# Retention, then a swish MLP, on one core: batch 0 in two-position runs and 64x64 tiles, its keys ahead of its values

## The chip, the cores and the metric

The kernel runs on one core of a Trainium2 chip. TensorE (PE) multiplies matrices out of SBUF into PSUM; VectorE (DVE) and ScalarE (ACT) read PSUM; GpSimd (POOL) works on SBUF alone; SyncE (SP) issues most of the DMAs. Each engine takes its instructions in order. The metric is device time in microseconds, the median of several runs. The profile shows one execution.

## What is computed

```python
scores = scale * np.matmul(q, k.transpose(0, 1, 3, 2))
gamma = 1.0 - 2.0 ** (-5.0 - np.arange(H, dtype=np.float32))
rel = pos[:, None] - pos[None, :]
Dmat = np.where(rel >= 0, gamma[:, None, None] ** rel[None, :, :], 0.0)
attn = np.matmul(scores * Dmat[None], v)
x = attn.transpose(0, 2, 1, 3).reshape(B * S, H * D)
h = x @ w_in
out = (h * (1.0 / (1.0 + np.exp(-beta * h)))) @ w_out
```

There are 8 batches of 8 heads, 576 positions and 64 channels per head, all in float32. The decay gamma^(i-j) is a product of gamma^i on the query side and gamma^-j on the key or value side, so no decay matrix is needed, only a causal mask. `w_in` is 512 x 2048 and `w_out` 2048 x 512, 4 MB each.

## The kernel before

Each batch has four chunks of 128 positions and a tail of 64; the tails of two batches are handled together. A chunk `c` works with keys and values of 128 positions on the 128 partitions. It has scores of the chunk's queries against its keys (`a_sc`, then a masking multiplication on DVE into `R`), values weighted by `R` (`a_O`), a crossing term from the running key-value state of all earlier chunks (`a_cross`), and an update of that state (`a_st`, with two ACT copies per chunk into the block-diagonal tiles `sbds`). `a_x` copies the result `O` out of PSUM into `xT`, transposed as the MLP needs it. Before that, queries are scaled with their decay (`pre_q`, tile `qs`) and transposed on PE (`t_q`, then a copy to `qT`); keys are cast to bf16 (`pre`, tile `kn`) and transposed (`t_k`, then an ACT copy to `kT`); values are scaled with gamma^-j (`pre`, tile `vn`, on POOL).

The queries are interleaved: partition p holds positions 4p to 4p+3, so a run of 4 x 64 floats, 1 KB, lies together in memory. Keys and values have one position per partition and run, 256 bytes. The kernel's first lines issue on SP's queue the queries of batch 0 (two halves of the heads, line 80), then the eight key and value loads of batch 0 (`ahead`, line 93), then `w_in` in pieces (`load_w_in`, line 177): four 256 columns wide, two 512 wide. A piece is cast to bf16 by `cast_w_in` (line 185), partly on POOL, partly on DVE. Two 256-wide pieces share one of the four `wt` buffers. The loads of `w_out` (line 189) use these buffers again and so wait for the casts.

The MLP of a batch is 16 `up` steps (line 410: four 512-column matmuls, then a Silu on ACT) and 16 `down` steps for each of four row blocks (line 423). The order of all work is written out by hand. First comes a straight list of calls for batch 0's attention, from line 454 on, with `warm_up` matmuls between them that compute nothing used. Then `merged` walks through the list `fill` of `up` and `down` steps of all batches and puts the attention steps of later batches, the casts and the loads between them at given places (`streams`). Every engine follows this order of program.

PSUM has eight banks, shared by tags: three `mm` (MLP, `warm_up`, some others), two `sc` (scores), two `O` (outputs, and the transposes `T`), one `st` (state). A new tile of a tag waits until an old one of that tag has been read.

## Time and profile before

| what | value |
|---|---|
| median of 3 runs | 312.85 us (312.38 to 313.4) |
| the profiled execution's span, first to last instruction | 310.4 us |
| the same execution's time outside the span | not listed; the median is 2.45 us above the span |
| PE busy | 299.4 us, 96% of the span |
| ACT, DVE, POOL busy | 46%, 35%, 31% |
| chain that ended last: PE, SP's queue, DMA | 89%, 4%, 3% |
| first `up` matmul | 19.51 us |
| granted TensorE clock | 1.000 |

The chain that ended last is followed back from the last instruction; its shares say what the time hung on. A line of the list in order of time has start, duration, engine, line, operation, what it writes and reads, and in brackets how long the engine had been idle and what ended that. In the windows, each engine has its busy time in the stretch, with the number of instructions.

### The profile page before, as it was taken

Reading aid. Unit: us, or ns where it says so; the run is one execution under the profiler, and the core shown is the slowest. Engines: PE = TensorE matmul, PEld = TensorE weight load, DVE = VectorE, ACT = ScalarE, POOL = GpSimd, SP = SyncE. Lnnn points to the kernel's source line nnn. Section 1 sums busy time; section 2 is a strip of 40 time slices with the busy share of each in tenths; the row PEclk is TensorE's granted clock in tenths of the full one; section 3 lists DMA queues with packets and bytes.
Section 4 is the critical chain, followed back from the end, with each engine's and each line's share of the span. In section 5 each row is a group of like instructions: output and inputs, shape, how many; then the busy total and the mean of one; then the engine's idle time right before and its main releaser. Section 6 shows DMA issues by size and latency. Waiting matters only on the chain.

```text
span 310.4 us, 5341 instructions
## 1 busy us (share of the span) xinstructions
PE 299.4 (96%) x2142; PEld 157.3 (51%) x2177; DVE 110.1 (35%) x196; ACT 141.5 (46%) x250; POOL 96.4 (31%) x131
## 2 busy tenths in 40 slices
PE   7789999999999999999999999999999999999996
PEld 5544456765454454445544544545455454444444
DVE  6554476342433142434431434133415420010012
ACT  5577626984147502661077106720574037206700
POOL 4663026846524281362228021912420000000000
PEclk9999999999999999999999999999999999999999
DMA  7999999999979989996989598949832110041011
GB/s 202 220 354 386 380 239 269 234 233 200 234 163 170 215 183 230 230 204 98 243 228 112 120 211 224 194 100 208 195 60 50 68 70 0 9 93 37 0 67 71
DMA packets 123897, 52.79 MB, mean 170 GB/s; under 512 B 105680, under 2 KB 116320, under 8 KB 123872
## 3 DMA queue, kind: packets, MB, share of 16 engines
q1 hardware_dynamic: 98496, 46.15, 61.3%
q10 hardware_dynamic: 25376, 6.30, 13.5%
q8 instruction: 17, 0.28, 0.4%
q14 instruction: 8, 0.07, 0.1%
HBM read 36.71 MB, written 9.44 MB: 149 GB/s over the span
## 4 chain that ended last, share of the span: by engine, by line
PE 89%; SPq 4%; DMA 3%; issue 1%; DVE 1%; ACT 0%
PE po L423 40%; PE ph L410 38%; DMA wt<-in_moe_w_in_dram 3%; SPq L93 3%; PE O L364 3%; PE sc L322 3%; PE O L350 2%; PE st L393 2%; SPq L177 1%; PE T L296 1%; PE T L302 1%; DVE xT L381 0%; DVE w_in_sb L185 0%; PE O L347 0%; SPq L80 0%
## 5 line engine op out<-in xcount | busy, mean ns | idle before, releaser
L412 ACT ACTIVATE gT<-ph,beta_sb 128x512 bf16<-128x512 f32 (+1 forms) x154 | 100.4, 659 | 83.1 <-PE ph L410 82.4
L410 PE MATMUL ph<-xT,w_in_sb 128*128 128x512 bf16 (+1 forms) x599 | 128.9, 365 | 2.5 <-DVE w_in_sb L185 1.1
L423 PE MATMUL po<-w_out_sb,gT 128*128 128x512 bf16 (+2 forms) x590 | 127.4, 368 | 1.3 <-issue 0.5
L410 PEld LDWEIGHTS <-w_in_sb 128*128 128x128 bf16 x616 | 58.7, 98 | 64.3 <-DVE w_in_sb L185 2.2
L423 PEld LDWEIGHTS <-gT 128*128 128x128 bf16 x608 | 57.0, 98 | 62.3
L332 DVE TENSOR_TENSOR R<-sc,causal 128x512 bf16<-128x512 f32 x71 | 44.3, 684 | 56.5 <-PE sc L322 55.0
L430 DVE COPY ot<-po 128x512 f32<-128x512 f32 (+2 forms) x38 | 25.0, 662 | 86.2 <-PE po L423 83.4
L254 POOL TENSOR_TENSOR vn<-kvn,gv 128x512 bf16<-128x512 f32 x32 | 33.3, 1042 | 16.8 <-DMA kvn<-in_v_dram 15.5
L272 POOL CAST kn<-kvn 128x512 bf16<-128x512 f32 x32 | 19.6, 612 | 58.9 <-DMA kvn<-in_k_dram 58.5
L246 POOL TENSOR_TENSOR qs<-qn,gq 128x512 bf16<-128x512 f32 x24 | 24.3, 1042 | 27.3 <-DMA qn<-in_q_dram 27.3
L381 DVE CAST xT<-O 128x512 bf16<-128x512 f32 x30 | 19.4, 687 | 34.8 <-PE O L350 15.5
L398 ACT CAST sbd<-st 64x256 bf16<-64x256 f32 x48 | 17.5, 364 | 18.8 <-PE st L393 16.6
L398 ACT CAST end<-st 64x256 bf16<-64x256 f32 x16 | 5.9, 366 | 29.4 <-PE st L393 29.3
L393 PE MATMUL st<-vn,kn 128*128 128x128 bf16 x128 | 12.4, 220 | 0.2 <-POOL vn L254 0.2
L364 PEld LDWEIGHTS <-vn 128*64 128x64 bf16 x288 | 8.7, 110 | 6.7 <-issue 6.1
L364 PE MATMUL O<-R,vn 128*64 128x128 bf16 x288 | 11.9, 223 | 0.0
L303 ACT COPY kT<-T 128x512 bf16<-128x512 bf16 x12 | 6.9, 586 | 8.8 <-PE T L302 7.7
L393 PEld LDWEIGHTS <-kn 128*128 128x128 bf16 x128 | 9.0, 98 | 3.5
L322 PE MATMUL sc<-qT,kT 64*128 64x128 bf16 x256 | 10.3, 218 | 0.4 <-ACT kT L303 0.2
L322 PEld LDWEIGHTS <-kT 64*128 64x128 bf16 x288 | 8.1, 94 | 3.8 <-ACT kT L303 1.5
L350 PE MATMUL O<-qT,sbd 128*128 128x128 bf16 x96 | 8.3, 221 | 0.3 <-ACT xT L381 0.2
L207 PE MATMUL ph<-warm 128*128 128x128 f32 (+1 forms) x24 | 6.9, 426 | 1.2 <-DVE warm L118 1.2
(56 smaller groups left out, 85.8 us busy)
## 6 DMA issues: line engine op xcount, KB each, us to landing
qn<-in_q_dram SPq DMA_DIRECT2D x16, 512.0 KB, 5.5
kvn<-in_k_dram SPq DMA_DIRECT2D x32, 256.0 KB, 5.9
kvn<-in_v_dram SPq DMA_DIRECT2D x32, 256.0 KB, 5.7
out_dram<-ot SPq DMA_DIRECT2D x31, 256.0 KB, 2.8
wt<-in_moe_w_out_dram SPq DMA_DIRECT2D x4, 1024.0 KB, 9.5
wt<-in_moe_w_in_dram SPq DMA_DIRECT2D x4, 512.0 KB, 7.3
wt<-in_moe_w_in_dram SPq DMA_DIRECT2D x2, 1024.0 KB, 11.7
out_dram<-ot SPq DMA_DIRECT2D x9, 128.0 KB, 2.4
```

The costliest lines, as they stand in the source:

```text
L246: e.tensor_tensor(batch[b]["qs"][:, cs, hs], q_tiles[b][:, hs, cs].rearrange("p h i d -> p i h d"), gq[:, cs, hs].unsqueeze(3).to_broadcas ...
L254: nc.gpsimd.tensor_tensor(live[i]["vn"][:], kv_tiles.pop(i)[:, 1], gains(gv, c), ALU.mult)
L272: nc.gpsimd.tensor_copy(kn[:, c % 2], t[:, 0])
L322: nc.tensor.matmul(view(sc[j][:, p, :]), L["kT"][r, p, :], rhs, start=True, stop=True, skip_group_check=True)
L332: nc.vector.tensor_tensor(R[:, j], sc[j][:], causal4[:] if i == CB - 1 else m_b, ALU.mult)
L364: nc.tensor.matmul(O[j * D:(j + 1) * D, p, :], vn[:, 2 * p + j, :], R[:, j, p, :], start=p == 0 and not (early and crossed), stop=early or ...
L393: nc.tensor.matmul(st[:, p, :], heads(L["kn"], p), heads(L["vn"], p), start=(c == 0 and p == 0), stop=True, skip_group_check=True)
L398: nc.scalar.copy(s[r, :, j * D:(j + 1) * D], st[r, :, j * D:(j + 1) * D])
L410: nc.tensor.matmul(ph, w_in_sb[:, ko, fo * P:(fo + 1) * P], xts[m][:, ko, :, w], start=(ko == 0), stop=(ko == KO - 1))
L412: nc.scalar.activation(gts[m][:, fo, :, w], ph, ACT.Silu, scale=beta_sb[:, fo:fo + 1])
L423: nc.tensor.matmul(po[:, :nn], gT[:, fo, ms, :], w_out_sb[:, fo, n0:n0 + nn], start=(fo == 0), stop=(fo == FO - 1))
L430: nc.vector.tensor_copy(ot, po[:, :nn])
```

## The change

The queries of batch 0 come in halves with a quarter of the keys between them. Keys and values of batch 0 are loaded in two spans of 256 positions, two positions to a partition (512-byte runs), each in two halves of the heads: all keys first, then all values. The decay gamma^-j moves from the values to the keys of batch 0. Since a partition now holds two positions, a chunk's keys lie on 64 partitions in two layers, and scores, outputs and states of batch 0 work on half of the partitions: 64x64 tiles for scores and outputs. The order of batch 0's attention is written anew. `betas_safe` and the reciprocal move from POOL to DVE, ahead of the queries. The first 256 columns of `w_in` come in two pieces; the last state of batch 0 (`w_st(3)`) goes into the stream behind the first `up` step. The qT copies of batch 0 change between DVE and ACT. Special forms for batch 0 in `a_sc`, `a_cross` and `a_O` go. The diff, with the set-up of constants and the removed branches shortened:

```diff
-    ahead = [(0, 0), (0, 1), (1, 0), (1, 1), (2, 0), (3, 0), (2, 1), (3, 1)]
+    SP = 2 * P
+    wide = {}
+    def load_q0(u):
+        if u == 0:
+            q_tiles[0] = stage.tile([P, H, CB, D], F32, name="qn", tag="qn", bufs=2)
+        w = slice(u * HP, (u + 1) * HP)
+        nc.sync.dma_start(q_tiles[0][:, w].rearrange("p h i d -> p h (i d)"),
+                          q[0, w, :MB, :].rearrange("h (p i) d -> p h (i d)", i=CB))
+    def load_wide(s, j, u):
+        if u == 0:
+            wide[s, j] = stage.tile([P, H, 2, D], F32, name="kvn", tag="kvn", bufs=NQ)
+        w = slice(u * HP, (u + 1) * HP)
+        nc.sync.dma_start(wide[s, j][:, w].rearrange("p h i d -> p h (i d)"),
+                          (k, v)[j][0, w, s * SP:(s + 1) * SP, :].rearrange("h (p i) d -> p h (i d)", i=2))
...
-    load_q(0)
-    for n, j in ahead:
-        load_kv(n, (j,))
+    load_q0(0)
+    load_wide(0, 0, 0)
+    load_q0(1)
+    for s, j, u in ((0, 0, 1), (1, 0, 0), (1, 0, 1), (0, 1, 0), (0, 1, 1), (1, 1, 0), (1, 1, 1)):
+        load_wide(s, j, u)
...
+    nc.gpsimd.iota(pos[:, 2 * CV:], pattern=[[SP, 2], [1, 2]], base=0, channel_multiplier=2,
+                   allow_small_or_imprecise_dtypes=True)
...
-    causal4 = consts.tile([P, HP, P], BF16, name="causal4")
-    nc.gpsimd.tensor_copy(causal4[:], causal[:].unsqueeze(1).to_broadcast([P, HP, P]))
+    causal_w = consts.tile([P, 2, P], BF16, name="causal_w")
+    nc.gpsimd.memset(causal_w[:], 1.0)
+    for x in range(2):
+        for i in range(2):
+            r = slice(x * TL, (x + 1) * TL)
+            nc.gpsimd.affine_select(out=causal_w[r, i], in_=causal_w[r, i], pattern=[[1, CB], [CB, PC]],
+                                    compare_op=ALU.is_ge, fill=0.0, base=-i, channel_multiplier=-2)
...
-    pieces = [(f, 256) for f in range(0, 1024, 256)] + [(f, 512) for f in range(1024, d_ff, 512)]
+    pieces = [(0, 128), (128, 128)] + [(f, 256) for f in range(256, 1024, 256)] + [(f, 512) for f in range(1024, d_ff, 512)]
...
-            on_pool = ko == KO - 1 or g < 4 and ko > 1
+            on_pool = ko == KO - 1 or g < 5 and ko > 1
...
-        nc.gpsimd.tensor_tensor(tiny[:], beta_sb[:], beta_sb[:], ALU.mult)
-        nc.gpsimd.tensor_scalar(tiny[:], tiny[:], 1e-24, 1e-12, ALU.is_lt, ALU.mult)
-        nc.gpsimd.tensor_tensor(beta_sb[:], beta_sb[:], tiny[:], ALU.add)
+        nc.vector.tensor_tensor(tiny[:], beta_sb[:], beta_sb[:], ALU.mult)
+        nc.vector.tensor_scalar(tiny[:], tiny[:], 1e-24, 1e-12, ALU.is_lt, ALU.mult)
+        nc.vector.tensor_tensor(beta_sb[:], beta_sb[:], tiny[:], ALU.add)
+        nc.vector.reciprocal(rbeta_sb[:], beta_sb[:])
...
-        (nc.vector.tensor_copy if u else nc.scalar.copy)(batch[b]["qT"][:, :, 2 * u:2 * u + 2], T[:])
+        (nc.vector.tensor_copy if u != (b == 0) else nc.scalar.copy)(batch[b]["qT"][:, :, 2 * u:2 * u + 2], T[:])
...
+    def wide_start():
+        t = sb.tile([P, 12, HP, P], BF16, name="w0", tag="gT", bufs=2)
+        for s in range(2):
+            spans[s] = dict(
+                kn=sb.tile([P, 2, H, D], BF16, name="kn", tag="kn", bufs=4),
+                kT=sb.tile([P, 2, HP, P], BF16, name="kT", tag="kT", bufs=4),
+                vn=t[:, 8 + 2 * s:10 + 2 * s].rearrange("p i g (t d) -> p i (g t) d", t=2),
+                R=[t[:, 4 * s + 2 * u:4 * s + 2 * u + 2].rearrange("p j (i g) s -> p j i g s", i=2) for u in range(2)])
+            for x in range(2):
+                live[2 * s + x] = {}
+    def w_k(s, u):
+        w = slice(u * HP, (u + 1) * HP)
+        g = gv[:, CV + 2 * s:CV + 2 * s + 2, w].unsqueeze(3).to_broadcast([P, 2, HP, D])
+        nc.gpsimd.tensor_tensor(spans[s]["kn"][:, :, w], wide[s, 0][:, w].rearrange("p h i d -> p i h d"), g, ALU.mult)
+    def w_v(s, u, copy):
+        w = slice(u * HP, (u + 1) * HP)
+        copy(spans[s]["vn"][:, :, w], wide[s, 1][:, w].rearrange("p h i d -> p i h d"))
+    def w_tk(s, u):
+        T = psum.tile([P, 2, 2, P], BF16, name="T", tag="O", bufs=2)
+        for i in range(2):
+            for g in range(2):
+                nc.tensor.transpose(T[:, i, g, :], heads(spans[s]["kn"][:, i], 2 * u + g), ident[:])
+        nc.scalar.copy(spans[s]["kT"][:, :, 2 * u:2 * u + 2], T[:])
+    def w_sc(s, u):
+        tag = "mm" if u else "sc"
+        sc = [psum.tile([P, 2, 2, P], F32, name="sc", tag=tag, bufs=3 if u else 2) for _ in range(2)]
+        for g in range(2):
+            for i in range(2):
+                for x in range(2):
+                    for j in range(2):
+                        r = slice(j * D, (j + 1) * D)
+                        p, c = 2 * u + g, 2 * s + x
+                        nc.tensor.matmul(sc[j][x * D:(x + 1) * D, i, g, :].rearrange("k (i s) -> k i s", i=CB),
+                                         spans[s]["kT"][r, i, p, x * D:(x + 1) * D],
+                                         batch[0]["qT"][r, :, p, c * PC:(c + 1) * PC],
+                                         start=True, stop=True, skip_group_check=True)
+        m_b = causal_w[:].unsqueeze(2).to_broadcast([P, 2, 2, P])
+        for j in range(2):
+            nc.vector.tensor_tensor(spans[s]["R"][u][:, j], sc[j][:], m_b, ALU.mult)
+    def w_O(s, u):
+        for x in range(2):
+            if u == 0:
+                live[2 * s + x]["O"] = psum.tile([P, HP, P], F32, name="O", tag="sc" if s else "O", bufs=2)
+        for g in range(2):
+            for i in range(2):
+                for x in range(2):
+                    for j in range(2):
+                        r, p = slice(x * D, (x + 1) * D), 2 * u + g
+                        nc.tensor.matmul(live[2 * s + x]["O"][j * D:(j + 1) * D, p, :],
+                                         spans[s]["vn"][r, i, 2 * p + j, :], spans[s]["R"][u][r, j, i, g, :],
+                                         start=p == 0 and i == 0, stop=False, skip_group_check=True)
+    def w_st(c):
+        s, r = c // 2, slice(c % 2 * D, (c % 2 + 1) * D)
...
+        for p in range(HP):
+            for i in range(2):
+                nc.tensor.matmul(st[:, p, :], heads(spans[s]["kn"][r, i], p), heads(spans[s]["vn"][r, i], p),
+                                 start=(c == 0 and p == 0 and i == 0), stop=True, skip_group_check=True)
+        t = ends[0] if c == CB - 1 else sbds[c % NS]
+        for j in range(2):
+            r = slice(j * D, (j + 1) * D)
+            (nc.vector.tensor_copy if j and c == 2 else nc.scalar.copy)(t[r, :, j * D:(j + 1) * D], st[r, :, j * D:(j + 1) * D])
...
-    warm_up(5)
+    wide_start()
+    warm_up(3)
     betas()
     betas_safe()
...
+    warm_up(2)
+    pre_q(0, 0)
+    pre_q(0, 1)
+    w_k(0, 0)
     t_q(0, 0)
+    w_tk(0, 0)
+    w_k(0, 1)
     warm_up(1, 128)
+    w_sc(0, 0)
+    pre_q(0, 2)
+    pre_q(0, 3)
+    w_k(1, 0)
     t_q(0, 1)
+    w_tk(0, 1)
+    w_k(1, 1)
     warm_up(1, 128)
+    w_sc(0, 1)
+    w_tk(1, 0)
+    w_v(0, 0, nc.gpsimd.tensor_copy)
     warm_up(1, 128)
+    w_sc(1, 0)
+    w_tk(1, 1)
+    w_O(0, 0)
+    w_v(0, 1, nc.scalar.copy)
+    w_v(1, 0, nc.gpsimd.tensor_copy)
+    w_v(1, 1, nc.gpsimd.tensor_copy)
+    w_st(0)
+    w_O(0, 1)
+    w_sc(1, 1)
+    w_st(1)
+    a_cross(1)
+    w_O(1, 0)
+    a_x(0)
+    a_cross(2)
+    w_st(2)
+    w_O(1, 1)
+    a_x(1)
+    a_x(2)
+    a_cross(3)
+    a_x(3)
     cast_w_in(0)
     cast_w_in(1)
-    nc.vector.reciprocal(rbeta_sb[:], beta_sb[:])
...
-    streams = [[(0, F(load_w_out, 0)), (1.1, F(cast_w_in, 2)), (3.1, F(cast_w_in, 3)), (3.2, F(load_w_out, 1)),
-                (6.1, F(cast_w_in, 4)), (6.2, F(load_w_out, 2)), (10.1, F(cast_w_in, 5)), (10.2, F(load_w_out, 3))],
+    streams = [[(0.1, F(load_w_out, 0)), (0.2, F(cast_w_in, 2)), (0.3, F(w_st, 3)), (1.1, F(cast_w_in, 3)),
+                (3.1, F(cast_w_in, 4)), (3.2, F(load_w_out, 1)), (6.1, F(cast_w_in, 5)), (6.2, F(load_w_out, 2)),
+                (10.1, F(cast_w_in, 6)), (10.2, F(load_w_out, 3))],
```

## The prediction, made before the changed kernel ran

> **What bounds the kernel now.** I read the windows first (who is busy when), then the list of instructions in order of time for the first 20 us, then the chain that ended last.
>
> The windows of the kernel before; the last three figures are TensorE's granted clock, the DMA share and GB/s:
>
> ```profile
> 4.50:5.00 0.50, 0.50 (x3) 0.41 (x2) 0.00 (x0) 0.17 (x1) 0.00 (x0) 1.00 1.09 387
> 9.50:10.00 0.50, 0.38 (x8) 0.28 (x9) 0.00 (x0) 0.07 (x1) 0.50 (x1) 1.00 1.38 220
> 18.00:18.50 0.50, 0.50 (x12) 0.40 (x12) 0.00 (x0) 0.47 (x1) 0.00 (x0) 1.00 1.09 344
> 24.00:24.50 0.50, 0.50 (x4) 0.24 (x3) 0.08 (x1) 0.32 (x2) 0.33 (x1) 1.00 1.06 389
> ```
>
> These are queries (1 KB runs, 387 GB/s), keys and values (256-byte runs, 220), narrow weight pieces (1 KB runs, 344) and wide ones (2 KB, 389). The DMA engines never rest before 40 us, and the short runs cost them almost half their rate.
>
> The list in order of time of the kernel before (start, duration, engine, line):
>
> ```profile
> 5.12 1.29 DVE L246 TENSOR_TENSOR qs<-qn,gq 128x512 bf16<-128x512 f32 x2 [0.73 <-DMA qn<-in_q_dram]
> 6.62 1.31 DVE L246 TENSOR_TENSOR qs<-qn,gq 128x512 bf16<-128x512 f32 x2 [0.21 <-DMA qn<-in_q_dram]
> 6.91 1.01 ACT L297 COPY qT<-T 128x1024 bf16<-128x1024 bf16 x1 [1.06 <-PE T L296]
> 7.88 0.61 POOL L272 CAST kn<-kvn 128x512 bf16<-128x512 f32 x1 [0.49 <-DMA kvn<-in_k_dram]
> 8.98 0.58 ACT L303 COPY kT<-T 128x512 bf16<-128x512 bf16 x1 [1.06 <-PE T L302]
> 9.08 1.04 POOL L254 TENSOR_TENSOR vn<-kvn,gv 128x512 bf16<-128x512 f32 x1 [0.59 <-DMA kvn<-in_v_dram]
> 12.45 1.29 DVE L332 TENSOR_TENSOR R<-sc,causal 128x512 bf16<-128x512 f32 x2 [1.04 <-PE sc L322]
> 14.26 0.74 ACT L398 CAST sbd<-st 64x256 bf16<-64x256 f32 x2
> 18.91 0.80 POOL L185 CAST w_in_sb<-wt 128x256 bf16<-128x256 f32 x2 [1.63 <-DMA wt<-in_moe_w_in_dram]
> 19.18 0.37 ACT L379 CAST xT<-O 128x256 bf16<-128x256 f32 x1 [0.71 <-DVE xT L378]
> 19.51 0.39 PE L410 MATMUL ph<-xT,w_in_sb 128*128 128x512 bf16 x1 [0.51 <-DVE w_in_sb L185]
> ```
>
> The first `up` matmul runs at 19.51. The weights landed at 18.9; attention's last copy ends at 19.55. So both end together, and a gain needs both earlier.
>
> The chain that ended last, before (start, duration, what):
>
> ```profile
> 15.30 10.77 DMA wt<-in_moe_w_in_dram
> 26.10 1.19 DVE w_in_sb L185 x2
> ...
> 34.31 8.63 PE po L423 x40
> ...
> 47.74 0.55 PE sc L322 x16
> ...
> 50.57 0.57 PE O L364 x16
> ```
>
> From 34.3 us TensorE carries the chain almost alone (PE 89% of it), one 512-column matmul in 8.63/40 = 0.216 us. Batch 0's `up` has 64 of these, 13.84 us, and took 34.31 - 19.51 = 14.80: 0.96 us waited for weights, mostly the piece that landed at 26.1. So everything that moves the end is the start of `up`, call it S, plus stalls behind it. The execution's span is 310.4; the median of the three runs is 312.85, so 2.45 lie around it, and I add the difference to the median.
>
> **The loads.** Keys and values of batch 0 are 2.10 MB: 9.5 us at 220 GB/s. The trace has no load in 512-byte runs. Bounds: 220 (256-byte row) and 387 (1 KB row). Per engine of 16 a 256-byte run takes 18.6 ns and a 1 KB run 42.3; midway by size, 512 bytes take 26.5 ns, 309 GB/s, 6.8 us: 2.7 saved (0 to 4.1). The two 128-wide pieces, 0.52 MB, leave the 344 rate (1.5 us) for something between 220 and 344; 1.8, a loss of 0.3. So the piece of 26.1 lands near 23.7, the first one, also half as large, near 15.5. The Trainium skill, "DMA: Bandwidth & Descriptors", Specifications, puts the least transfer for line rate at 512 B; by that the upper bound holds and the saving is 4.1, which, as the next part shows, moves S by only 0.2 us. Nothing here shows that rule at 512 B.
>
> **What attention now waits for.** I lay out each engine's queue in program order, with the durations above. Latencies: four transposes to the copy 0.43 (8.55 to 8.98); copy to scores 0.06 (9.56 to 9.62); DVE to PE 0.12; a group's last matmul to its reader 0.20. New forms: a scores or output step of 16 64x64 matmuls. Bounds: 0.40, the streaming floor of the two-tile form, to 16 x 0.055 = 0.88, whole-array matmuls in line (four transposes take 0.22). I take the nearest rows, 16 half-array matmuls in 0.55 (scores) and 0.57 (outputs), from the chain's two lines. Eight half-height state matmuls 0.44; value copy on ACT 0.65 (the 128x512 copies run 0.58 to 0.72).
>
> - First query half lands at 5.1. The key quarter behind it: 1.26 at most (before, 6.62 to 7.88), 0.7 at 387 GB/s; 6.2. The beta chain, now ahead of the queries on DVE, bounds 5.1 to 5.9 for them; not later than the key's way. Scaling a key quarter on POOL 1.04 (was a 0.61 cast), then 0.06 + 0.43 + 0.58 + 0.06: scores at 8.4.
> - Scores 0.55 + 0.20, mask on DVE 9.1 to 10.4. DVE runs in order, so the second query half, landed near 7.5, is scaled only now: 1.29, to 11.7. Before, it was scaled at 6.62.
> - Transposes 0.12 + 0.44, qT on ACT 1.01 (DVE and ACT change places), kT behind it on ACT 0.58, 0.06: second scores at 13.9. Before, the third chunk's were at 14.4.
> - kT, scores, kT again: in PE's order each transpose stands behind the scores before it. 0.55 + 0.43 + 0.58 + 0.06 = third scores at 15.5; 0.55 + 0.43 + 0.58 = last kT at 17.1.
> - The first outputs need two "O" banks, and the last kT's T holds one: 17.2. All four blocks' value sums start only here. ACT copies v to 17.75; first state 17.8, its two ACT copies (0.74) 18.45 to 19.2; PE meanwhile runs the second outputs and the last scores (to 19.35), second state; copies 20.0 to 20.7; crossing and third state to 21.45; copies 21.65 to 22.0 (one on DVE); last crossing to 22.4.
> - ACT's queue behind that: xT of block 1 22.0, of block 2 22.6, its half of block 3 23.2 to 23.55. DVE's half ends at 23.0, its first cast 0.2 later. `up` starts at 23.3 and its third matmul waits to 23.6: S = 23.2 in effect.
>
> The same layout of the old queues gives 19.8 where the trace has 19.51, so I take 0.3 off: S = 22.9. With all bounds in favour (387 GB/s, 0.45 per step, latency 0.16) it is 22.1; with 220 GB/s 23.2.
>
> The Trainium skill, "TensorEngine Tiling (Array Packing)", Performance Considerations, says tiling speeds TensorE but not the emptying of PSUM. The DVE row agrees in kind: a mask pair took 1.29 after scores of 0.27. The page's four-fold tiles would, as an estimate, run a step in 0.21 and give S near 22.0, still late.
>
> **What else moves.** POOL: one iota, one memset, four selects for `causal_w` less the 0.61 copy, about 1 us more, ending near 4.8, before the first key lands; then 4 x 1.04 + 3 x 0.61 = 6.0 us against 6.6, off the path. The pieces have all landed when S comes: `up` 8 at S + 6.9 = 29.8 against 23.7 + 1.2; so the 0.96 us of stalls go. Without that cover (S below 18.0) the piece would again set the pace. `w_st(3)` goes into the `up` stream: 8 x 0.055 = 0.44 on PE, where before the last state ran ahead of `up`; its two ACT copies have the 0.17 us that ACT idles per `up`. On SP, the first `w_out` load now waits for three casts, to about S + 1.3 = 24.2, against 21.37. The queue behind it (three `w_out` loads, then batch 1's queries, keys, values) starts later too, and the DMA engines pause about 1.5 us; it lands near 30 (2.7 us for 1 MB at 389 GB/s, some 3 to start and land), needed at S + 14.3 = 37.2; the others 2.7 us apart against a need 2.6 apart, also covered. A missed one would cost up to 2.7. Batch 1's loads follow near their old times, their users 3 us later. From batch 1 on nothing changes.
>
> Sum: S + 13.84 + 0.44 = 37.2 against 34.31: +2.9 us. 312.85 + 2.9 = 315.7, 0.9% slower.
>
> **Rivals.** First, faster: attention keeps pace with the data, and the weights set S. The eighth `up` then needs 23.7 + 1.2 = S + 6.9, S = 18.0, and the sum is 18.0 + 14.28 - 34.31 = -2.0: 310.8. For it: the DMA engines are the visible limit before 19 us, and by the rates above the last values land near 14. Against: it needs the second scores at about 9, before the second query half is even scaled. It decides at S = 20.0; below that the change is faster.
>
> Second, no difference: two of the long waits (second half behind the first mask, first outputs behind the last kT) turn out shorter, since the order of issue leaves more overlap than I see. S = 20.0, 312.8. Against: both are in-order queues, and the old one fits the layout within 0.3.
>
> Third, 64x64 matmuls stream one after another: 0.88 a step. Laid out again, S is 2.1 later: 317.8. For: the loads of 128x64 weights take 110 ns against 94 for 64x128. Against: both forms ran 16 in 0.55 to 0.57.
>
> Fourth, the clock: between 9.1 and 13.9 PE has only some 1.3 us of work. If that halved its clock until `up`, about 3 us of matmuls on the chain would double: 318.7. Against: every window of the trace grants 1.00, with PE busy 69% of 12 to 14 us.
>
> The loads not getting faster is no separate case: S moves 0.3.
>
> **How the numbers follow.** Main case 0.70, own range 314.5 to 316.8 (S 21.7 to 24.0); faster 0.12, since the schedule is worked out for tiles that the trace doesn't hold; no difference 0.07; serial tiles 0.07; clock 0.04. A measurement tells from no change about 0.3%, 0.94 us. Faster 0.12, same 0.07, slower 0.81. The range reaches from the second rival to the third and leaves out the first and the clock (0.16): 312.8 to 317.8.
>
> **What would show it.** Right: keys and values at 280 to 340 GB/s; DVE's second pair of `qs` directly behind the first mask pair, near 10.4; second scores near 14; first outputs behind the last kT copy; first `up` at 22 to 24, then 64 `up` matmuls with no wait for weights. Wrong: `qs` of the second half before the first mask; `up` before 20 us; `up` waiting for DMA; steps of 16 longer than 0.7 us; a clock below 1.00.

## The result and the profile after

The changed kernel takes 323.49 us (median of six executions, 321.92 to 324.07), the kernel before 312.81 beside it: ratio 1.0327, 95% interval 1.0304 to 1.0351. That is 10.7 us slower, where +2.9 was forecast. Ratios here and below leave disturbed executions out; where a kernel's times spread with its clock (a1 and c1 below), a ratio can therefore lie below that of the medians.

The page of the changed kernel: the span, and TensorE's busy time and granted clock in tenths over 40 equal slices of 8.05 us.

```profile
span 322.0 us, 5492 instructions
...
PE   7498999999999999999999999999999999999995
...
PEclk9655899999999999999999999999999999999999
```

Before, the clock row held nothing but nines. Now slices two to five do not, and from the sixth on the two kernels look alike: all of the loss is made before about 45 us. The windows of the changed kernel put numbers on that stretch (length, busy time of PE, PEld, DVE, ACT and POOL with instruction counts, granted clock, DMA share, GB/s):

```profile
9.00:10.00 1.00, 0.42 (x16) 0.26 (x16) 0.29 (x2) 0.14 (x1) 1.00 (x2) 1.00 1.17 291
10.00:12.00 2.00, 0.00 (x0) 0.00 (x0) 2.00 (x3) 0.00 (x0) 2.00 (x3) 0.59 1.17 290
12.00:20.00 8.00, 6.16 (x75) 4.41 (x76) 3.77 (x6) 3.19 (x5) 5.00 (x14) 0.50 1.11 333
20.00:27.00 7.00, 6.52 (x100) 4.69 (x97) 1.75 (x4) 3.38 (x8) 1.97 (x4) 0.50 0.66 244
27.00:34.80 7.80, 7.00 (x23) 2.96 (x25) 5.19 (x20) 3.17 (x6) 0.00 (x0) 0.54 0.58 182
34.80:40.00 5.20, 5.20 (x26) 2.35 (x24) 1.52 (x4) 4.05 (x6) 0.00 (x0) 1.00 1.04 394
```

PE did nothing from 9.62 to 12.24 us, while DVE and POOL were busy without a break; its clock halved at 10.36 and was full again only at 34.25. A busy PE at clock 0.50 is a slow PE, not a loaded one: it got 23 matmuls into 7.80 us, and 26 into the next 5.20.

The list in order of time of the changed kernel (start, duration, engine, line, operation; in brackets the idle time before and what ended it) shows why PE stood still:

```profile
5.77 2.07 DVE L274 TENSOR_TENSOR qs<-qn,gq 128x512 bf16<-128x512 f32 x2
5.88 1.41 POOL L415 TENSOR_TENSOR kn<-kvn,gv 128x512 bf16<-128x512 f32 x1 [1.23 <-DMA kvn<-in_k_dram]
...
8.59 3.04 POOL L415 TENSOR_TENSOR kn<-kvn,gv 128x512 bf16<-128x512 f32 x3 [1.30 <-DMA kvn<-in_k_dram]
...
9.20 0.42 PE L438 MATMUL sc<-qT,kT 64*64 64x128 bf16 x16 [0.40 <-ACT kT L426]
...
9.73 1.29 DVE L444 TENSOR_TENSOR w<-sc,causal_w 128x512 bf16<-128x512 f32 x2 [0.71 <-PE sc L438]
10.94 2.26 DVE L274 TENSOR_TENSOR qs<-qn,gq 128x512 bf16<-128x512 f32 x2
...
12.24 0.61 PE L324 MATMUL T<-ident,qs 128*128 128x128 bf16 x4 [2.62 <-DVE qs L274]
...
27.58 0.61 PE L501 MATMUL ph<-xT,w_in_sb 128*128 128x512 bf16 x1 [0.65 <-DVE w_in_sb L212]
```

The second query pair stands directly behind the first mask pair in DVE's queue, as forecast. But it takes 2.26 us, and the first pair 2.07, where a pair took 1.29 and 1.31 before. POOL multiplies keys beside the first pair and the start of the second, and casts values beside the rest. It is slower too: 1.41 for its first multiplication, against 1.04, and 1.07 for the cast at 11.58, against 0.61; its multiplications beside DVE's mask keep their 1.04. Scores of 16 64x64 matmuls took 0.42 at full clock. The chain that ended last, from the first `up` matmuls on (start, duration, what), answers to the chain of before, where the first `down` matmul began at 34.31:

```profile
28.41 1.06 PE ph L501 x2
29.47 0.96 PE st L467 x8
30.43 10.43 PE ph L501 x39
40.91 4.48 PE ph L501 x20
45.39 6.26 PE po L514 x29
```

The first `down` began 11.1 us later than before, and that is the loss (some 0.4 us come back outside the span: 1.7 us lie there, against 2.1 to 2.2 before). 8.1 of it is the later first `up` (27.58 against 19.51). The other 3.0 is a longer `up`: 17.8 us instead of 14.8. (The list in order of time has both first `down` matmuls 0.16 earlier than the chain, at 45.23 and 34.15; the differences are the same.)

### The profile page after: what moved, and what is told of

Same layout as the page of the kernel before. It is cut to its first block, busy times and chain, and to the rows that moved or that the text cites. A ratio compares the mean times of both kernels' runs of the same rounds, so it can differ in the third digit from the quotient of the medians.

```text
span 322.0 us, 5492 instructions
## 1 busy us (share of the span) xinstructions
PE 307.8 (96%) x2214; PEld 162.1 (50%) x2249; DVE 111.1 (34%) x202; ACT 140.6 (44%) x249; POOL 95.4 (30%) x134
## 3 DMA queue, kind: packets, MB, share of 16 engines
q10 hardware_dynamic: 25376, 6.30, 13.9%
## 4 chain that ended last, share of the span: by engine, by line
PE 92%; DVE 3%; ACT 2%; issue 1%; POOL 0%; POOLq 0%; ACTq 0%; DVEq 0%
PE ph L501 39%; PE po L514 39%; PE O L382 3%; PE sc L350 3%; PE O L371 2%; PE st L484 2%; DVE qs L274 1%; PE st L467 1%; PE T L324 1%; ACT kT L426 1%; PE sc L438 1%; PE O L456 1%; PE T L330 0%; ACT gT L503 0%; DVE xT L396 0%
## 5 line engine op out<-in xcount | busy, mean ns | idle before, releaser
L501 PE MATMUL ph<-xT,w_in_sb 128*128 128x512 bf16 (+1 forms) x599 | 131.5, 370 | 2.4 <-DVE w_in_sb L212 0.9
L355 DVE TENSOR_TENSOR R<-sc,causal 128x512 bf16<-128x512 f32 x64 | 39.7, 683 | 52.9 <-PE sc L350 52.9
L300 POOL CAST kn<-kvn 128x512 bf16<-128x512 f32 x28 | 17.1, 610 | 71.2 <-DMA kvn<-in_k_dram 71.0
L282 POOL TENSOR_TENSOR vn<-kvn,gv 128x512 bf16<-128x512 f32 x28 | 29.2, 1042 | 14.6 <-DMA kvn<-in_v_dram 10.2
L489 ACT CAST sbd<-st 64x256 bf16<-64x256 f32 x42 | 15.3, 364 | 17.9 <-PE st L484 15.5
L484 PE MATMUL st<-vn,kn 128*128 128x128 bf16 x112 | 10.8, 219 | 0.0
L382 PE MATMUL O<-R,vn 128*64 128x128 bf16 x256 | 10.2, 222 | 0.0
L350 PE MATMUL sc<-qT,kT 64*128 64x128 bf16 x224 | 8.7, 217 | 0.1
L324 PE MATMUL T<-ident,qs 128*128 128x128 bf16 x48 | 4.7, 241 | 3.9 <-DVE qs L274 3.9
L325 ACT COPY qT<-T 128x1024 bf16<-128x1024 bf16 x3 | 3.0, 1012 | 12.2 <-PE T L324 12.2
## 6 DMA issues: line engine op xcount, KB each, us to landing
wt<-in_moe_w_in_dram SPq DMA_DIRECT2D x2, 1024.0 KB, 10.7
```

The lines of the kernel that those rows point to most:

```text
L282: nc.gpsimd.tensor_tensor(live[i]["vn"][:], kv_tiles.pop(i)[:, 1], gains(gv, c), ALU.mult)
L350: nc.tensor.matmul(view(sc[j][:, p, :]), L["kT"][r, p, :], rhs, start=True, stop=True, skip_group_check=True)
L355: nc.vector.tensor_tensor(R[:, j], sc[j][:], m_b, ALU.mult)
L382: nc.tensor.matmul(O[j * D:(j + 1) * D, p, :], vn[:, 2 * p + j, :], R[:, j, p, :], start=p == 0, stop=b is not None and c == 0, skip_group ...
L484: nc.tensor.matmul(st[:, p, :], heads(L["kn"], p), heads(L["vn"], p), start=(c == 0 and p == 0), stop=True, skip_group_check=True)
L489: nc.scalar.copy(s[r, :, j * D:(j + 1) * D], st[r, :, j * D:(j + 1) * D])
```

## The experiments

The theory after this first look: the stop at 9.6 us and the gaps just ahead of it halve the clock, and the slow clock costs some 6 us on the chain; contention between DVE and POOL and the order in DVE's queue cost the rest. The rivals: the loads, the 64x64 tiles, or the narrow pieces are to blame, or the clock is only a symptom that costs nothing by itself.

**a1_warm: matmuls that compute nothing, in the largest gap and in a later one.**

```diff
     w_sc(0, 0)
+    warm_up(3)
     pre_q(0, 2)
...
     w_tk(0, 1)
     w_k(1, 1)
+    warm_up(1)
     warm_up(1, 128)
     w_sc(0, 1)
```

> The changed kernel with idle matmuls put into TensorE's two longest gaps: three of 256 columns after the first scores, one more before the second scores. Theory 1 (the halved clock is a price of its own, on top of a late chain): the clock stays at 1.00, matmuls of up take 0.216 us from the start, the first up comes near 25.0 instead of 27.6, the first down near 39.5 instead of 45.4, and the time is near 317.5 us. Theory 2 (the chain is late whatever the clock, and the low clock only goes with it): time within 1 us of 323.5. Theory 3 (the filler itself delays work on PE): slower than 323.5.

Measured 320.62 us, ratio 1.0225 (1.0146 to 1.0305). The four executions spread with their mean clock: 318.15 at 0.995, 318.82 at 0.989, 322.42 at 0.979, 323.39 at 0.973. So the clock was not held: in the profiled execution it was half from 8.24 to 11.65 and again from 25.30 to 28.72. The direction fits the theory and the size did not. Two gaps filled are not all the gaps.

**a2_warm_plain_keys: POOL only casts the keys.** a1 with the key decay left out of the computation, so that POOL reads one tile instead of two:

```diff
-        nc.gpsimd.tensor_tensor(spans[s]["kn"][:, :, w], wide[s, 0][:, w].rearrange("p h i d -> p i h d"), g, ALU.mult)
+        nc.gpsimd.tensor_copy(spans[s]["kn"][:, :, w], wide[s, 0][:, w].rearrange("p h i d -> p i h d"))
```

> As the filled kernel, but POOL only casts the keys of batch 0 (one input from SBUF) and leaves out their decay, so the output is not the reference's. Theory 1 (DVE's query scaling and POOL's key scaling, both with two inputs from SBUF, hold each other up): the two pairs of query scalings on DVE go from 2.07 and 2.26 us back to about 1.3 each, the second scores come 1.5 to 2 us earlier, and the time is 1.3 to 2 us below the filled kernel's. Rival (DVE's scaling is slow because of something else, the clock or the DMA traffic): the pairs stay near 2.1 us and the time differs by less than 0.5 us, all of it from POOL's shorter casts.

Measured 317.57 us, ratio 1.0150 (1.0093 to 1.0207); 317.32 and 315.99 in the two executions at clock 1.00. The list in order of time of a2:

```profile
5.90 0.96 POOL L415 CAST kn<-kvn 128x512 bf16<-128x512 f32 x1 [1.25 <-DMA kvn<-in_k_dram]
...
6.31 1.09 DVE L274 TENSOR_TENSOR qs<-qn,gq 128x512 bf16<-128x512 f32 x1
...
10.50 1.79 DVE L274 TENSOR_TENSOR qs<-qn,gq 128x512 bf16<-128x512 f32 x2
```

The expectation was half met. The DVE operation that starts beside POOL's cast takes 1.09, against 1.52 beside its multiplication and 0.69 in the kernel before; the cast takes 0.96 against 0.61. So the two engines hold each other up, and a cast does it too, only for less time. The pairs take 1.64 and 1.79, not 1.3.

**a3_warm_queries_first: the second query half ahead of the first mask.** a1 with two `warm_up` matmuls in place of three and

```diff
-    w_sc(0, 0)
     pre_q(0, 2)
     pre_q(0, 3)
+    w_sc(0, 0)
+    warm_up(2)
```

> As the filled kernel, but DVE scales the second half of the queries ahead of the first mask pair (two idle matmuls instead of three behind the first scores). Theory 1 (DVE's order holds the second scores back): the second scores start near 13.5 instead of 15, and the time is 1 to 1.8 us below the filled kernel's. Rival (something behind it sets the end, the chain of key transposes and ACT's queue): less than 0.4 us.

Measured 316.93 us, ratio 1.0126 (1.0085 to 1.0168), in executions from 315.75 to 319.14. The clock still wandered (0.983 to 0.999), and the times do not follow it in order (315.75 at 0.995, 317.02 at 0.999), so this run does not say what the order alone is worth; a6 below does.

**b1_no_filler: the kernel before, without its own filler.** All `warm_up(n, 128)` calls in batch 0's attention are left out of the kernel before.

```diff
     t_q(0, 0)
-    warm_up(1, 128)
     t_q(0, 1)
...
     t_k(0)
-    warm_up(2, 128)
     a_sc(0)
```

> The kernel before without the idle matmuls between its attention steps (the five at the start stay). Theory 1 (the clock falls when PE has too little to do over some microseconds): the record shows a clock below 1.00 before 35 us, and the time is 2 to 5 us above 312.8. Rival (only a full stop of PE of more than 2 us, as in the changed kernel, lowers the clock; the old kernel has none): clock 1.00 throughout and a time within 0.5 us of 312.8.

Measured 313.11 us, ratio 1.0003 (0.9988 to 1.0017): no difference, though the clock did fall. Windows of b1:

```profile
10.00:11.00 1.00, 0.45 (x7) 0.30 (x6) 0.85 (x2) 0.34 (x1) 0.80 (x2) 1.00 1.35 219
11.00:12.00 1.00, 1.00 (x12) 0.73 (x12) 0.44 (x1) 0.77 (x3) 0.48 (x1) 0.50 1.39 220
...
14.00:15.00 1.00, 1.00 (x20) 0.64 (x18) 0.19 (x1) 0.97 (x3) 0.54 (x1) 0.80 1.39 221
```

It was half from 10.99 to 14.41, where attention still waits for keys and values at 220 GB/s. This bounds the theory: here the half clock ended inside a stretch limited by transfers, and it cost nothing. What costs is a half clock on the chain.

**a5_full_filler: filler in all the gaps.** a1, and in `t_q` and the later calls

```diff
             for p in range(2):
                 nc.tensor.transpose(T[:, i, p, :], heads(batch[b]["qs"][:, i], 2 * u + p), ident[:])
+            if b == 0 and i == 2:
+                warm_up(1, 128 if u else 256)
...
     w_tk(1, 1)
+    warm_up(1, 128)
...
     a_x(0)
+    warm_up(1, 128)
...
     a_x(2)
+    warm_up(1, 128)
     a_cross(3)
     a_x(3)
+    warm_up(1, 128)
```

> The changed kernel with idle matmuls in all of TensorE's gaps before up (within the query transposes, behind the first scores, ahead of the second scores and of the first outputs, around the last crossing). Theory 1 (the halved clock is what the filled kernel's slower executions still pay): the clock stays at 1.00 to the end of up in the profiled execution, up needs 13.9 to 14.5 us from its first matmul to the first down, the first up is near 24.5, and the time is 316.5 to 318 with executions within 1 us of each other. Rival (executions differ for another reason): clock 1.00, but times still spread over 3 us or more.

Measured 317.78 us (317.43 to 318.08), ratio 1.0150 (1.0132 to 1.0168). The clock was 0.997 to 1.0 and the spread 0.65 us. Windows of a5, in stretches of the table above:

```profile
10.00:12.00 2.00, 2.00 (x18) 1.33 (x10) 1.62 (x3) 0.00 (x0) 1.98 (x3) 1.00 1.17 290
...
20.00:27.00 7.00, 6.03 (x81) 3.91 (x80) 4.61 (x17) 4.28 (x10) 1.71 (x4) 1.00 0.77 258
27.00:34.80 7.80, 7.77 (x36) 3.53 (x36) 3.02 (x9) 6.19 (x10) 1.78 (x1) 1.00 0.93 336
```

and its list in order of time:

```profile
15.18 0.42 PE L440 MATMUL sc<-qT,kT 64*64 64x128 bf16 x16 [0.66 <-ACT kT L428]
...
24.32 0.39 PE L503 MATMUL ph<-xT,w_in_sb 128*128 128x512 bf16 x1 [0.38 <-DVE w_in_sb L212]
...
39.14 6.21 PE L516 MATMUL po<-w_out_sb,gT 128*128 128x512 bf16 x28
```

The added matmuls compute nothing that is used, and they take 5.7 us off. From the last `kT` copy to the first `up` it is 6.35 us (17.97 to 24.32), where the changed kernel took 8.46 (19.12 to 27.58). `up` takes 14.82 instead of 17.65 (27.58 to 45.23 by the list). 317.78 is what the change costs without the clock: +5.0 us. It is at most that, since filler stands on a5's own chain too (0.96 us at 7.07, 0.28 at 12.98 and 0.42 at 21.11).

**a4_narrow_loads: 256-byte runs again.** a5, with each of the wide loads issued as two, one for each position:

```diff
-        nc.sync.dma_start(wide[s, j][:, w].rearrange("p h i d -> p h (i d)"),
-                          (k, v)[j][0, w, s * SP:(s + 1) * SP, :].rearrange("h (p i) d -> p h (i d)", i=2))
+        for i in range(2):
+            nc.sync.dma_start(wide[s, j][:, w, i],
+                              (k, v)[j][0, w, s * SP:(s + 1) * SP, :].rearrange("h (p i) d -> i p h d", i=2)[i])
```

> The kernel with filler in all gaps, its keys and values loaded in 256-byte runs, one layer of the two positions per DMA, into the same places. Theory 1 (the loads are not what attention waits for): keys and values run near 220 GB/s instead of 290, the last values land about 2.5 us later, the first up comes at most 0.6 us later, and the time is within 0.8 us of the fully filled kernel's. Rival (the 512-byte runs carry a gain that the rest of the change eats up): 2 to 2.5 us slower than the fully filled kernel.

Measured 318.04 us, ratio 1.0155 (1.0131 to 1.0180), against 317.78 of a5 on the same chip. The list in order of time of a4:

```profile
16.62 0.62 POOL L422 CAST w<-kvn 128x512 bf16<-128x512 f32 x1 [0.70 <-DMA kvn<-in_v_dram]
...
24.99 1.04 PE L504 MATMUL ph<-xT,w_in_sb 128*128 128x512 bf16 x3 [0.54 <-DVE w_in_sb L213]
```

The last value quarter comes 2.8 us later (16.62; 13.79 in a5) and the first `up` 0.7 later, and 0.3 us of time is left of it, with intervals that overlap. In this order of work, the faster loads buy next to nothing.

**a6_full_queries_first: a3's order at a full clock.** a5 with a3's edit.

> The changed kernel with filler in all gaps and DVE scaling the second half of the queries ahead of the first mask pair. Against the fully filled kernel (317.78), with the clock at 1.00 in both: if DVE's order holds the chain back, second scores near 14 instead of 15.2 and 1.0 to 1.5 us less, 316.3 to 316.8; if the key transposes behind it set the end anyway, less than 0.4 us.

Measured 315.89 us (315.25 to 316.35), ratio 1.0080 (1.0053 to 1.0107). The list in order of time of a6:

```profile
9.15 2.80 DVE L274 TENSOR_TENSOR qs<-qn,gq 128x512 bf16<-128x512 f32 x2
...
14.00 0.42 PE L440 MATMUL sc<-qT,kT 64*64 64x128 bf16 x16 [0.66 <-ACT kT L428]
...
23.27 1.04 PE L503 MATMUL ph<-xT,w_in_sb 128*128 128x512 bf16 x3 [0.38 <-DVE w_in_sb L212]
```

The second scores come 1.2 us earlier than in a5 and the first `up` 1.05 earlier; the time falls by 1.9, with one filler matmul less. So the place of the second query half in DVE's queue costs 1 to 2 us. The pair itself became longer still (2.80): each of its two multiplications now starts beside one of POOL's key multiplications.

**b2_narrow_pieces: the first pieces alone, in the kernel before.**

```diff
-    pieces = [(f, 256) for f in range(0, 1024, 256)] + [(f, 512) for f in range(1024, d_ff, 512)]
+    pieces = [(0, 128), (128, 128)] + [(f, 256) for f in range(256, 1024, 256)] + [(f, 512) for f in range(1024, d_ff, 512)]
...
-            on_pool = ko == KO - 1 or g < 4 and ko > 1
+            on_pool = ko == KO - 1 or g < 5 and ko > 1
```

with the casts in `streams` renumbered for seven pieces.

> The kernel before with one part of the change alone: the first 256 columns of w_in in two pieces of 128. Theory 1 (attention and weights end together, so a half-size first piece gains nothing, and its 512-byte runs delay the later pieces): up starts within 0.3 us of 19.5, the wait for the piece that landed at 26.1 grows by 0.2 to 0.4 us, time 312.9 to 313.5. Rival (the first piece is the limit): up starts 0.4 to 0.6 us earlier and the time is 312.3 to 312.6.

Measured 312.91 us, ratio 1.0000 (0.9990 to 1.0010). The first `up` came 0.29 us earlier (19.22), but the piece that `up` waits for landed 0.4 later (26.50 against 26.10, as expected). `up` stood still for its casts until 27.00 and again until 27.76 (once, until 27.34, in the kernel before), and `down` began 0.42 later (34.57 against 34.15 by the lists). The time is the same because 0.4 us less lies outside the span (1.7 against 2.1 to 2.2), with this edit alone; why was not found. On balance the pieces are neither gain nor loss there.

**c1_reordered: everything that the chain waits for in attention, put in another order.** The loads, tiles and pieces of the change stay. The first keys of span 1 are loaded right behind the second query half, ahead of the other keys of span 0; the decay goes back to the values; all queries are scaled ahead of any mask; all scores run ahead of any output; `betas_safe` moves behind the scores; `w_st(3)` stands ahead of `up`. Two of the three `warm_up(1, 128)` between the steps go, and one `warm_up(1)` comes in behind the last scores.

```diff
-    for s, j, u in ((0, 0, 1), (1, 0, 0), (1, 0, 1), (0, 1, 0), (0, 1, 1), (1, 1, 0), (1, 1, 1)):
+    for s, j, u in ((1, 0, 0), (0, 0, 1), (1, 0, 1), (0, 1, 0), (0, 1, 1), (1, 1, 0), (1, 1, 1)):
...
-        nc.gpsimd.tensor_tensor(spans[s]["kn"][:, :, w], wide[s, 0][:, w].rearrange("p h i d -> p i h d"), g, ALU.mult)
+        nc.gpsimd.tensor_copy(spans[s]["kn"][:, :, w], wide[s, 0][:, w].rearrange("p h i d -> p i h d"))
...
-        copy(spans[s]["vn"][:, :, w], wide[s, 1][:, w].rearrange("p h i d -> p i h d"))
+        nc.gpsimd.tensor_tensor(spans[s]["vn"][:, :, w], wide[s, 1][:, w].rearrange("p h i d -> p i h d"), g, ALU.mult)
...
-        tag = "mm" if u else "sc"
+        tag = "mm" if s else "sc"
...
-            (nc.vector.tensor_copy if j and c == 2 else nc.scalar.copy)(t[r, :, j * D:(j + 1) * D], st[r, :, j * D:(j + 1) * D])
+            (nc.vector.tensor_copy if j and c < 3 else nc.scalar.copy)(t[r, :, j * D:(j + 1) * D], st[r, :, j * D:(j + 1) * D])
```

The calls, in their new order: `pre_q` 0 and 1, `w_k(0, 0)`, `t_q(0, 0)`, `w_tk(0, 0)`, `pre_q` 2 and 3, the other three `w_k`, `w_sc(0, 0)`, `w_tk(1, 0)`, `t_q(0, 1)`, `w_sc(1, 0)`, `w_tk(0, 1)`, `w_sc(0, 1)`, `w_tk(1, 1)`, `w_sc(1, 1)`, `betas_safe`, the values, and then outputs, states and crossings with `cast_w_in(0)` and `cast_w_in(1)` between them.

> The changed kernel's loads and 64x64 tiles in another order of attention: DVE scales all queries before the first mask; both spans' first head halves get their scores first; the decay goes back from the keys to the values (POOL casts keys, multiplies values after DVE has done the queries); the second halves of the state copies go to DVE; the last state runs ahead of up. Theory 1 (the order and the port shared by DVE and POOL made the change slow, not the tiles): second scores near 9.5, first up at 17.7 to 19.5, up then waits for weights only slightly, time 310.5 to 312.5. Rival (the small tiles or PSUM's banks make attention slow in any order): first up after 21, time above 314.

Measured 317.94 us (313.36 to 320.06, ten executions), ratio 1.0095 (1.0052 to 1.0137). The page of c1 shows that the new order fell into the same trap:

```profile
PEclk9558999999999999999999999999999999999999
```

The lowest time stands at a mean clock of 0.998, the highest at 0.968. In the profiled execution, at 0.973, the first `up` came at 24.50.

**c2_reordered_filled: c1 with filler.** `warm_up` gets a tag, so that filler can use the `st` bank while the `mm` banks hold scores:

```diff
-    def warm_up(n, cols=256):
-        ph = psum.tile([P, MB], F32, name="ph", tag="mm", bufs=3)
+    def warm_up(n, cols=256, tag="mm"):
+        ph = psum.tile([P, MB], F32, name="ph", tag=tag, bufs=3 if tag == "mm" else 1)
...
     w_sc(0, 0)
+    warm_up(1, tag="st")
...
     w_tk(0, 1)
+    warm_up(2, 128, tag="st")
...
     w_tk(1, 1)
+    warm_up(1, 128, tag="st")
     w_sc(1, 1)
-    warm_up(1)
+    warm_up(2, tag="st")
...
     w_O(0, 1)
+    warm_up(1, 128)
...
     w_O(1, 0)
+    warm_up(1, 128)
```

> The reordered kernel with idle matmuls in TensorE's gaps, most of them into the state's bank, which is free until the first state. Theory 1 (the halved clock is all that keeps the reordered kernel behind): clock 1.00 before up, first up between 17.7 and 19.5, time 310.5 to 312.5, executions within 1 us of each other. Theory 2 (the new order is itself late; its best executions near 313.4 are its floor): first up after 20, time 313 to 314.5.

Measured 313.57 us (312.61 to 315.47, twelve executions), ratio 1.0017 (1.0001 to 1.0033). The clock was 0.995 to 1.0, so the second theory holds: at a full clock too this order is late. The four scalings of c2, as one source line with least, median and largest ns, and below them the same line of the changed kernel:

```profile
L274 DVE TENSOR_TENSOR qs<-qn,gq x4: 681/684/691, 5.0 to 8.0; 128x512 bf16<-128x512 f32 x4
```

```profile
L274 DVE TENSOR_TENSOR qs<-qn,gq x4: 627/1166/1525, 5.8 to 12.1; 128x512 bf16<-128x512 f32 x4
```

POOL casts instead of multiplying, and its casts start behind DVE's scalings, not ahead of them: DVE is not held up, and the cast that starts beside one takes 0.88 instead of 0.61. The chain of c2:

```profile
13.56 1.06 PE ph L234 x4
14.62 0.35 PE O L456 x16
14.96 0.56 PE st L467 x8
15.55 0.38 ACT sbd L475
15.95 0.44 DVE sbd L475
...
20.54 13.96 PE ph L508 x64
34.50 9.50 PE po L521 x44
```

64 `up` matmuls run without a wait in 13.96 us, and `down` begins at 34.50 (34.31 before). Two costs are left on the chain: the filler itself (1.06 us at 13.56), and state copies of which DVE's half starts only when ACT's half has ended.

**c3_state_first: what the chain of c2 offers.** The first state runs ahead of the first outputs, in the place of the filler on the chain; both halves of a state copy go to ACT.

```diff
-            (nc.vector.tensor_copy if j and c < 3 else nc.scalar.copy)(t[r, :, j * D:(j + 1) * D], st[r, :, j * D:(j + 1) * D])
+            nc.scalar.copy(t[r, :, j * D:(j + 1) * D], st[r, :, j * D:(j + 1) * D])
...
-    warm_up(2, tag="st")
...
-    w_O(0, 0)
     w_st(0)
+    w_O(0, 0)
     w_O(0, 1)
-    warm_up(1, 128)
```

> The reordered, filled kernel with the chain of states shortened: the first state ahead of the first outputs and no idle matmuls before it (they stood 1.06 us on the chain), no idle matmuls between the first outputs and the second state, and all state copies on ACT (a half on DVE waited for the half on ACT). Theory 1 (three rounds of state, copy, state set the end): first up near 18.8 instead of 20.5, up without waits, first down near 32.7, time near 311.8, below the kernel before. Rival (the pieces of w_in or the masks on DVE set the end now): first up after 20 or up with waits of over 1 us, time 313 or more. If the clock falls for want of idle matmuls: executions that differ by over 2 us.

Measured 311.70 us (311.27 to 312.33, nine executions) against 313.01 of the kernel before on the same chip: ratio 0.9955 (0.9940 to 0.9971). It beats both kernels. The list in order of time of c3:

```profile
19.63 13.99 PE L508 MATMUL ph<-xT,w_in_sb 128*128 128x512 bf16 x62
33.45 6.85 PE L521 MATMUL po<-w_out_sb,gT 128*128 128x512 bf16 x31
```

The first `up` comes at 19.63, later than expected and no earlier than before (19.51), but nothing interrupts it, and `down` begins 0.70 us earlier than before (34.15 in that list). Of the rest of the 1.3 us, some 0.4 lies outside the span, as in nearly all the kernels here with the narrow pieces, b2 among them (1.7 us; a6 varies from 1.8 to 2.5). Which of c3's edits over c2 is worth what was not tried apart.

## Why the prediction was right and wrong

**Right: the sign, the chain and the reason why attention is late.** The sum "S + 13.84 + 0.44" holds within 0.7 once PE runs at its full clock: by the chain, `up` with its state took 14.98 in a5 (24.32 to 39.30; 0.5 of the 0.7 is `up` waiting for DVE's first casts), and 13.96 without the state in c2. The break-even at S = 20.0 fits c2 and c3 to about half a microsecond; they have no state in `up` and so break even 0.44 later: S of 20.51 gave 1.0017, 19.63 gave 0.9955. The second query half lay behind the first mask as forecast, and that place is worth 1 to 2 us (a6). That the loads move S little was right in kind: in a4 the narrow loads moved it by 0.7, where 0.3 was forecast, and the time by 0.3. The loads themselves ran at 290 GB/s, within the bounds but below the 309 taken. The Trainium skill, "DMA: Bandwidth & Descriptors", Specifications, has line rate from 512 B on; by that they should have run at the 387 of the 1 KB row, and the measurement decides against it here. The third rival, tiles in line, falls: 16 matmuls took 0.42, less than the 0.55 assumed (and twice the 0.21 that the prediction estimated for four tiles at once), and third scores followed the second by 1.42 in a5 where 1.6 was laid out. The narrow pieces are innocent in sum (b2).

**Wrong, 5.7 of the 7.8 us missed: the clock.** The step that failed is the setting aside of the fourth rival: the sum takes every matmul at the full clock. The rival named the place and the mechanism ("between 9.1 and 13.9 PE has only some 1.3 us of work"), and then failed twice. It was set aside because "every window of the trace grants 1.00". But the trace before had no such gap: its least busy microsecond between 4 and 15 held 0.47 us of work, the new kernel 2.6 us of none. A trace can't speak against what happens in a gap that it doesn't contain. (Only 0.74 us of the 2.6 lie ahead of the fall at 10.36. In the whole 3.41 us before it, smaller gaps included, PE was busy 42% of the time; cut in the same way, the kernel before has no such stretch under 74% in its first 45 us.) And the price ended too early: "until `up`". The clock stayed half to 34.25, 6.7 us into `up`. Measured against a5, whose own filler stands on its chain, the slow clock cost at least 1.15 us up to the last `kT` copy, 2.1 from there to the first `up`, and 2.8 within `up`: 6.1 to the first `down`, 5.7 in the medians. Of the prediction's own signs, the clock below 1.00 told that it was wrong, and the first `up` missed its 22 to 24.

**Wrong, the other 2.1 at most: three terms of the layout.** At a full clock the change costs up to +5.0 (a5), not +2.9. First, "1.29" for a query pair: DVE's scaling was priced from a trace where POOL ran only 16-column operations beside it. With POOL's key multiplications and casts there it had to wait for them (last section) and took 2.07 and 2.26, 0.8 and 1.0 more; a5, whose filler shifts the second pair, has 1.55. That the four key multiplications on POOL lie "off the path" was true of POOL's time and not of DVE's. Second scores, forecast at 13.9, came at 15.18 in a5. The faster tiles gave 0.4 back, so the last `kT` copy ended at 17.97 instead of 17.1 and the first `up` began at 24.32 instead of 23.3. Second, the casts that `up` waits for at its start: 0.5. Third, the 0.3 taken off because the old layout came out late by that much: the new one did not.

Step by step, in us from the span's start, by the lists (the forecast of the first `down` counts from the chain's 34.31, where the list has 34.15). In c3 the second scores are those of span 1's first half of the heads; the first that need the second query half start at 12.33.

| step | forecast | changed kernel | a5, full clock | c3 |
|---|---|---|---|---|
| first scores | 8.4 | 9.20 | 9.62 | 8.18 |
| second query half scaled | 11.7 | 13.20 | 13.13 | 9.30 |
| second scores | 13.9 | 15.45 | 15.18 | 10.90 |
| last `kT` copy ends | 17.1 | 19.12 | 17.97 | 13.69 |
| first `up` | 23.3 | 27.58 | 24.32 | 19.63 |
| first `down` | 37.2 | 45.23 | 39.14 | 33.45 |

The first rival, faster at S = 18.0, is not reached even by c3. Its condition, second scores near 9, was missed there too (10.90), and the start of `up` is then set by the states, not by weights.

## What to carry to other kernels

Before a change opens a gap on TensorE, or several small ones close together, ask what follows: a few empty microseconds can cost many at half the clock. Price that from the first gap to the end of the next densely filled stretch, not to the end of the gap, and do not take a trace without the gap as evidence. An operation moved to POOL is not free because POOL is idle; look at what DVE does in the same microseconds, and which of the two starts first. When a change loses, separate its parts before dropping it: here the same loads and tiles, in another order and with filler in the gaps, give 0.9955 of the old time.

## What the runs showed of the hardware

**The clock is granted in steps of 3.41 us.** In every profiled execution that lost it in batch 0, the time at half clock is a whole multiple of that: 3.41 (b1), 3.41 twice (a1), 3.41 (a3), 13.65 (a2; four steps), 17.07 (c1; five), 23.89 (the changed kernel; seven). Cut at these steps, the windows of the changed kernel show what decides:

```profile
6.95:10.36 3.41, 1.43 (x28) 0.96 (x26) 2.21 (x4) 0.58 (x1) 2.11 (x3) 1.00 1.16 295
10.36:13.77 3.41, 1.13 (x10) 0.87 (x11) 2.84 (x4) 0.00 (x0) 2.90 (x4) 0.50 1.17 290
...
20.60:24.01 3.41, 3.41 (x65) 2.58 (x64) 1.29 (x2) 1.95 (x5) 0.71 (x3) 0.50 1.04 381
...
30.84:34.25 3.41, 3.41 (x10) 1.21 (x9) 0.80 (x3) 1.31 (x3) 0.00 (x0) 0.50 0.86 305
```

A step in which PE was busy 1.43 of 3.41 us, 42%, was followed by the half clock. Over all these runs, the clock fell after steps with PE busy 42 to 64% of the time, and stayed full after steps with 59% and more; between 59 and 64% it went either way. At half clock it came back after steps busy 94 to 100%, and not after those with 33 to 90%; nor after three that were busy throughout with attention's small matmuls (20.60 to 24.01 above is one). That the small tiles count for less would explain the three, and was not tested. The Trainium skill, "TensorE: Matmul & The Clock Gate", Part 1, gives a free-running window of 3413 ns, with the half clock after an idle window and the full one after a busy window. The length agrees with these runs to the hundredth. "Idle" does not: no step here was idle, and 42 to 64% was little enough. A window that runs free of the kernel would also explain why one kernel's executions differ (a1: 318.15 to 323.39; c1: 313.36 to 320.06), depending on where its gaps fall.

**DVE and POOL take turns.** A 128x512 DVE multiplication with two operands in SBUF took 0.69 us in the kernel before, where POOL ran only 16-column operations beside it or started a cast at its end. It took up to 1.09 when it started beside a POOL cast and up to 1.52 when it started beside a POOL multiplication. POOL's multiplication took 1.41 instead of 1.04, and a cast 0.88 to 1.07 instead of 0.61. The list in order of time of the changed kernel, with DVE's first pair taken apart:

```profile
5.77 0.63 DVE L274 TENSOR_TENSOR qs<-qn,gq 128x512 bf16<-128x512 f32 x1
5.88 1.41 POOL L415 TENSOR_TENSOR kn<-kvn,gv 128x512 bf16<-128x512 f32 x1 [1.23 <-DMA kvn<-in_k_dram]
6.32 1.52 DVE L274 TENSOR_TENSOR qs<-qn,gq 128x512 bf16<-128x512 f32 x1
```

Whichever begins first is not slowed (0.63 at 5.77). The other one waits for its end: DVE's second ends at 7.84, 0.55 after POOL's at 7.29. The second pair repeats it: its two multiplications end at 12.18 and 13.20, 0.55 after POOL's at 11.63 and 12.65. In c2, where DVE's began first, only POOL's cast grew. So in these rows the price is what is left of the other engine's instruction, not a lower rate. The Trainium skill, "GPSIMD Engine Reference", Specifications, says that POOL shares its SBUF interfaces with VectorE and contends with instructions of two SBUF inputs; the rows agree, and give the price.

**Left open.** One of the six executions of the changed kernel took 321.92 us with a recorded clock of 1.00. By a5 it should have been near 318; there is no trace of it, so either the record or the reading is incomplete. Nor was it found why the DVE half of a split state copy waits for the ACT half (18.71 to 19.08 on ACT, then 19.11 to 19.54 on DVE in c2; the list names ACT's copy as what ended DVE's wait).
